# First unit's decays in two loads and two scans, unit 7's decays loaded once, other order numbers

## The chip, the cores and the metric

The kernel runs on one core of one Trainium2 chip. The core has five engines that run at the same time and wait for each other through semaphores: TensorE (PE in the profile), VectorE (DVE), ScalarE (ACT), GpSimd (POOL) and SyncE (SP, which here only issues DMAs). The metric is the device time of one execution in microseconds, as the median of the runs. Lower is better.

## The reference

A linear attention with a decaying state, and behind it a two-layer MLP with an ELU.

```
B, H, S, D = 4, 8, 768, 48
for t in range(S):
    cur = einsum('bhd,bhe->bhde', u[None] * kt, vt)
    y[:, :, t] = einsum('bhd,bhde->bhe', rt, state + cur)
    state = wt[:, :, :, None] * state + einsum('bhd,bhe->bhde', kt, vt)
x = y.transpose(0, 2, 1, 3).reshape(B * S, H * D)      # 3072 x 384
h = x @ w_in                                           # 384 x 2048
g = where(h > 0, h, exp(min(h, 0)) - 1)
out = g @ w_out                                        # 2048 x 384
```

The decays w lie between 0.8 and 0.95.

## The kernel before

**Units and chunks.** The 768 steps are cut into six chunks of 128 steps, each chunk into four units (24 units in all). A unit of the first chunk is one batch row with 128 steps and no state ahead of it ("whole"); a later one is two batch rows with 64 steps each. All eight heads of a unit lie in one tile: 112 partitions, four pairs of heads along the free side.

**What a unit does.** The names are those of the planner's tasks, in brackets the engine.

- `ld_w`, `ld_k`, `ld_v`, `ld_rk` (SP): the loads. w has 521 columns, k and r together 1024.
- `es` (DVE, L442): the running product of the decays from the end of each span of steps to its start, as one scan over reversed columns. The tile `reset` holds a 1 between the spans, so that each starts anew. `gs` (DVE, L451 and L452): the scan in the other direction, which starts from the reciprocals of what `es` ended with.
- `rkc` (DVE, L476): r times k, and `pd` (PE, L481): its product with u, the diagonal. `md` and `sp` (ACT) bring the diagonal into the tile `am`.
- `rh` (DVE, L457): "hats", k and r times the products of the decays, in place.
- `s` (PE, L522, L534, later L509): transposes and scores; `mk` (DVE, L546): the scores above the diagonal into `am`; `kt` (ACT).
- `v` (PE, L509, L574): outputs and the new state. Then `xf`, `xh` (ACT) and `xl` (DVE) make x for the MLP, split into two parts of fewer bits.
- `fl` (ACT, L461): checks each decay against 1, in place, and sums the result; a later branch uses it. For the units below `LATE` = 8, w is loaded once more for this (`ld_wx`) near the middle of the program, into a tile of its own; for the others `fl` runs on w itself, after `gs`, and w's buffer (of two) is held until then.

**The MLP.** Per chunk 16 steps of 128 hidden rows. A step is `g1` (PE, L262 or L266), `r1` and `r2` (ACT: relu and exp), the ELU's last operation (DVE, L276), `gh` (ACT) and `gl` (DVE, L284), and `g2` (PE, L294 or L297). The weights come as 64-bit numbers (`raw`, 768 KB for each of 16 loads) and are converted on chip: two ACT and two DVE operations (L632, L636), then a split into high and low part. The first six are used in the first chunk as they are (`w_f`), with fp32 matmuls of two passes each.

**What sets the order.** The program is put into tasks, and `Plan.order` walks through modelled time: on each engine it takes, of the tasks that are ready and whose buffers are free, the one with the earliest due time plus a number from the table `NUDGE`. The order in which tasks are taken is the order in which the instructions are issued; each engine keeps to it. `FILL` puts a number of products of a tile of ones (L416, into a PSUM bank that nothing reads) ahead of some PE tasks; they are no tasks and need no data.

SP issues each DMA on one of eight semaphores in turn; a ninth load waits until the first has landed.

```
LATE = 8
FILL = {("pd", 0): 15, ("s", 0): 6, ("pd", 1): 8, ("s", 1): 5, ("v", 1): 5, ("pd", 2): 1, ("g1", 2): 5}
```

Of the kernel before, what the change touches and what calls it, by code (L numbers as in the profile page):

```python
# [15 lines left out]
ALU = mybir.AluOpType  # L16
# [16 lines left out]
W1, K1, R1 = CWS + 1, NP * C, NP * C  # L33
WKR = dict(w=(0, W1), k=(W1, W1 + K1 + R1))
# [8 lines left out]
LOW = ['ACT']*16  # L43
RAWS = ["raw0", "raw1", "x1a", "x1b"] * 2 + ["raw0", "raw1"] * 4
DUE = {0: 9.0}
FILL = {("pd", 0): 15, ("s", 0): 6, ("pd", 1): 8, ("s", 1): 5, ("v", 1): 5, ("pd", 2): 1, ("g1", 2): 5}


def _pieces():
    res = []  # L50
    for h in range(H):
        s, e = h * D, (h + 1) * D
        while s < e:
# [16 lines left out]
DMA_FIRST, DMA_ISSUE, DMA_LAT, DMA_RATE = 1.8, 0.47, 1.0, 286.0  # L70
# [17 lines left out]
NUDGE = dict(a={1: -20.75, 2: -37.25},
             cc={1: -10, 2: -20.25, 6: 56.75, 8: -22, 11: 6, 12: 5.75, 14: -4.75, 15: 1.5},
             es={2: -12.5, 4: 3, 6: 3.5, 7: 13.5, 13: -11.5, 16: -1.75, 20: 3.75},  # L90
             g1={3: -1.25, 4: 21, 5: 16.5, 31: -17.25, 37: 70.75, 46: 48.25, 47: -20.75, 48: -0.5, 58: -15.25, 76: -6.25, 80: -9.25, 84: -11.5, 94: -11.75},
             g2={3: 88.5, 18: 4.25, 19: 14.25, 20: -1.5, 26: -11.5, 33: -5.25, 34: -2.75, 42: 0.25, 43: 6, 48: 24, 54: 7.5, 79: -12.75, 83: -8.5, 84: -17.5, 85: 16.75, 87: -4.25, 94: 6.75, 99: 51.75},
             ld={5: -17.75},
             raw={2: -71.5},
             rh={2: -16, 4: -9.75, 8: -40, 9: -5.5, 17: 42, 19: 17.75},
             s={1: -4.25, 12: 31.25, 17: 10},
             sp={1: 13.25, 6: 3.25, 13: -19.75, 19: -3.25, 23: -6},
             v={8: 24.25, 15: -15.5, 16: -18.25},
             wl={1: -22.25, 8: 15.75, 12: -2.25})
KIND = {n: k for k, v in LEADS.items() for n in v.split()}  # L100


class Plan:
# [5 lines left out]
    def add(self, key, eng, dur, fn, after=(), due=None, start=0.0, lock=False, size=0):  # L109
        self.tasks[key] = dict(key=key, eng=eng, dur=dur, fn=fn, after=list(after), due=due, start=start, lock=lock, size=size,  # L110
                               nudge=NUDGE.get(KIND.get(key[0]), {}).get(key[1] if len(key) > 1 else 0, 0.0))

# [215 lines left out]
def rwkv_elu_kernel(ctx, tc, wkr, rk, vp, u, uz, gkrw, gv, gu, wraw, out):  # L328
    nc = tc.nc
# [88 lines left out]
    def load_u(z):  # L418
        nc.sync.dma_start(ubd if z else ub, uz if z else u)

    def load(u_, n):
        i = u_["i"]
        if n in WKR:
            lo, hi = WKR[n]
            t, src = ld.tile([R2, hi - lo], F32, tag=n, name=n, bufs=SLOTS[n]), wkr[i, :, lo:hi]
        elif n == "wx":
            t, src = ld.tile([R2, W1], F32, tag=n, name=n, bufs=SLOTS[n]), wkr[i, :, 0:W1]
        elif n == "rk":
            t, src = ld.tile([P, 2, DM], F32, tag=n, name=n, bufs=SLOTS[n]), rk[i]
        else:  # L430
            t, src = ld.tile([P, 4 * P], F32, tag=n, name=n, bufs=SLOTS[n]), vp[i]
        nc.sync.dma_start(t, src)
        if n == "k":
            u_["k"], u_["r"] = t.rearrange("d (z p t) -> z d p t", z=2, p=NP)
            u_["kr"] = t.rearrange("d (z n) -> d z n", z=2)
        else:
            u_["w" if n == "wx" else n] = t

    def e_scan(u_):
        u_["eg"] = eg = at.tile([R2, 2, CWS + 1], F32, tag="eg", name="eg", bufs=SLOTS["eg"])  # L440
        n = u_["n"]
        nc.vector.tensor_tensor_scan(out=eg[:, 0, 0:n][:, ::-1], data0=u_["w"][:, 1:n + 1][:, ::-1], data1=reset[:, 0, 0:n][:, ::-1],  # L442
                                     initial=0.0, op0=ALU.mult, op1=ALU.max)

    def decay(u_):
        u_["pc"] = pcs[:, u_["i"], 0:NP * C // u_["L"]].unsqueeze(2)
# [232 lines left out]
    for u_ in units:  # L679
        i, c = u_["i"], u_["c"]  # L680
        early = max(0.0, BEGINS[c] - LEAD) if c > 0 else 0.0
        for n, kb in (("w", 274), ("k", 540), ("rk", 462), ("v", 308)):
            if n == "rk" and DIAG[i] == "PE":
                continue
            add(("ld_" + n, i), "SP", DMA_ISSUE, lambda u_=u_, n=n: load(u_, n), start=early, size=kb)
        again = i > 0 and units[i - 1]["whole"] != u_["whole"]
        if again:
            add(("reset", i), "POOL", 1.2, lambda u_=u_: set_reset(nc.gpsimd, u_), [("gs", i - 1)], lock=True)
        add(("es", i), "DVE", K["es"], lambda u_=u_: e_scan(u_), [("const",), ("ld_w", i)] + [("reset", i)] * again, lock=True)
        add(("gs", i), "DVE", K["gs"], lambda u_=u_: g_scan(u_), [("es", i)], lock=True)  # L690
        add(("rh", i), "DVE", K["hat"], lambda u_=u_: hats(u_), [("gs", i), ("ld_k", i)], lock=True)
        add(("pc", i), "ACT", K["pc"], lambda u_=u_: decay(u_), [("es", i)])
        if i < LATE:
            add(("ld_wx", i), "SP", DMA_ISSUE, lambda u_=u_: load(u_, "wx"), [("gs", i)], start=BEGINS[2] + 20.0, due=BEGINS[-3] + 4.0 * i, size=274)
        add(("fl", i), "ACT", K["fl"], lambda u_=u_: flag(u_), [("ld_wx", i)] if i < LATE else [("gs", i)], due=(BEGINS[-3] + 4.0 * i + 20.0) if i < LATE else None)
        if DIAG[i] == "PE":
            add(("rkc", i), "DVE", K["rh"], lambda u_=u_: r_k_rows(u_), [("ld_k", i)], lock=True)
            plan.tasks[("rh", i)]["after"].append(("rkc", i))
            add(("pd", i), "PE", K["pd"], lambda u_=u_: diag_pe(u_), [("rkc", i), ("ubd",)])
            add(("md", i), "ACT", K["md"], lambda u_=u_: diag_out(u_), [("pd", i)])  # L700
        else:
            e = DIAG[i]
            for n, fn, dep in (("rk", r_k, [("ld_rk", i)]), ("rku", r_k_u, [("rk", i), ("ub",)])):
                add((n, i), e, K[n if e == "DVE" else "p" + n],
                    lambda u_=u_, fn=fn, e=e: fn(u_, nc.vector if e == "DVE" else nc.gpsimd), dep, lock=True)
            add(("md", i), "DVE", K["dg"], lambda u_=u_: diag(u_), [("rku", i)])
        if SPREAD[i] == "ACT":
            add(("sp", i), "ACT", K["spa"], lambda u_=u_: spread_act(u_), [("md", i), ("const",)])
        elif SPREAD[i] == "DVE":
            add(("sp", i), "DVE", K["spd"], lambda u_=u_: spread_dve(u_), [("md", i), ("const",)], lock=True)  # L710
        else:
            add(("sp", i), "POOL", K["sp"], lambda u_=u_: spread(u_), [("md", i)], lock=True)
        before = []
        if not u_["whole"]:
            add(("sc", i), "DVE", K["sc"], lambda u_=u_: scale_state(u_), [("pc", i)] + [("up", x["i"]) for x in units[max(0, i - B):i - 1] if set(range(4)[x["b"]]) & set(range(4)[u_["b"]])], lock=True)
            before.append(("sc", i))
        add(("s", i), "PE", K["s0" if u_["whole"] else "s2" if u_["last"] else "s"], lambda u_=u_: score(u_), [("rh", i), ("const",)] + [("sp", i)] * (i > 1) + before, due=DUE.get(i))
        add(("mk", i), "DVE", K["mk0" if u_["whole"] else "mk"], lambda u_=u_: mask(u_), [("s", i), ("sp", i)])
        if not u_["last"]:
            add(("kt", i), "ACT", K["kt"], lambda u_=u_: trans_out(u_), [("s", i)])  # L720
        after = [("mk", i), ("kt", i), ("ld_v", i)]
        if i % B:
            after.append(("v", i - 1))
        add(("v", i), "PE", K["v0" if u_["whole"] else "v2" if u_["last"] else "v"], lambda u_=u_: value(u_), after,
            due=BEGINS[c] - (B - 1 - i % B) * (STAG if c > 1 else STAG1) - 2.0 if c else None)
        if u_["whole"]:
# [256 lines left out]
```

## Time and profile before

| | us |
|---|---|
| median of 3 runs | 508.84 (507.29 to 508.98) |
| the profiled execution, whole | 507.77 |
| its span, first to last instruction | 506.1 |
| ACT busy | 271.7 |
| POOL busy | 41.1 |

In the profile each row of the order in time gives start and length in us, engine, line, operation, what is written and read, and in brackets how long the engine was idle before it and what ended that. A PE row "x30" is 30 passes, since an fp32 product takes two passes. Landing times of DMAs are from issue to the last byte's signal. L416 to L636 are lines of the kernel before; behind line 421 the changed kernel's are 6 to 16 higher.

### The profile page before, as it was taken

How to read it: one execution, taken by the hardware profiler on the slowest of the kernel's cores; microseconds unless marked ns; L12 is line 12 of the kernel's file. 1: busy time of each engine (PE TensorE's matmuls, PEld its weight loads, DVE VectorE, ACT ScalarE, POOL GpSimd, SP SyncE). 2: the span in 40 equal slices, each digit the busy share in tenths (PEclk: the TensorE clock that was granted, in tenths of full speed). 3: DMA queues.
4: the chain of work that ended last, by engine and by line, in shares of the span. 5: the costliest groups of instructions: out<-in, count | busy, mean ns of one | idle time of the engine just before them, and what ended most of it. 6: DMA issues, size and time to landing. Idle time of an engine off the chain costs nothing.

```text
span 506.1 us, 13786 instructions
## 1 busy us (share of the span) xinstructions
PE 499.9 (99%) x6038; PEld 412.7 (82%) x6038; DVE 338.7 (67%) x509; ACT 271.7 (54%) x526; POOL 41.1 (8%) x54
## 2 busy tenths in 40 slices
PE   9999999999999999999999999999999999999996
PEld 8988888887888788888788888888888887888885
DVE  7999999996998423899432899433799543333332
ACT  4989576647554425656544545344645444445352
POOL 2000000013111100112000031100021100000000
PEclk9999999999999999999999999999999999999999
DMA  8967946104813100844290242320332000100001
GB/s 261 354 203 243 301 116 204 68 5 151 234 50 97 51 3 1 242 128 129 65 264 5 81 132 60 100 69 8 115 99 60 3 0 5 63 3 0 1 0 66
DMA packets 18738, 51.09 MB, mean 101 GB/s; under 512 B 2288, under 2 KB 2416, under 8 KB 18672
## 3 DMA queue, kind: packets, MB, share of 16 engines
q1 hardware_dynamic: 18240, 49.36, 32.6%
q8 instruction: 49, 0.80, 0.7%
q10 hardware_dynamic: 432, 0.79, 0.4%
q14 instruction: 17, 0.14, 0.1%
HBM read 45.42 MB, written 4.72 MB: 99 GB/s over the span
## 4 chain that ended last, share of the span: by engine, by line
PE 89%; DVE 6%; DMA 2%; issue 1%; ACT 1%; POOL 0%; DVEq 0%; ACTq 0%; POOLq 0%
PE acc L297 35%; PE ph L266 34%; PE pa L509 6%; PE acc L416 3%; PE acc L294 3%; PE ph L262 2%; PE pa L534 2%; PE pa L574 2%; DMA wx<-in_wkr_dram 2%; PE pb L522 1%; DVE eg L442 1%; DVE m L276 1%; DVE eg L452 0%; PE pb L481 0%; DVE gl L284 0%
## 5 line engine op out<-in xcount | busy, mean ns | idle before, releaser
L276 DVE SCALAR_TENSOR_TENSOR m<-m,ph 128x512 f32<-128x512 f32 (+2 forms) x104 | 66.3, 639 | 84.2 <-ACT m L273 84.0
L270 ACT ACTIVATE m<-ph 128x512 f32<-128x512 f32 (+2 forms) x104 | 58.5, 563 | 94.7 <-PE ph L266 86.7
L266 PE MATMUL ph<-xh,w_l 128*128 128x512 f32 x270 | 105.3, 390 | 0.0
L297 PE MATMUL acc<-gh,w_l 128*128 128x512 f32 x268 | 104.5, 390 | 0.0
L284 DVE TENSOR_TENSOR gl<-m,gh 128x512 fp32r<-128x512 f32 x90 | 62.4, 694 | 41.6 <-ACT gh L280 41.3
L280 ACT CAST gh<-m 128x512 fp32r<-128x512 f32 x90 | 55.7, 619 | 52.0 <-DVE m L276 29.6
L297 PE MATMUL acc<-gh,w_h 128*128 128x512 f32 x180 | 71.8, 399 | 0.0
L266 PE MATMUL ph<-xh,w_h 128*128 128x512 f32 x180 | 71.3, 396 | 0.0
L297 PE MATMUL acc<-gl,w_h 128*128 128x512 f32 x180 | 70.2, 390 | 0.0
L266 PE MATMUL ph<-xl,w_h 128*128 128x512 f32 x180 | 70.1, 390 | 0.0
L273 ACT ACTIVATE m<-m 128x512 f32<-128x512 f32 (+2 forms) x104 | 62.2, 600 | 2.1
L266 PEld LDWEIGHTS ph<-xh,w_l 128*128 128x128 f32 x270 | 50.7, 188 | 10.7
L297 PEld LDWEIGHTS acc<-gh,w_l 128*128 128x128 f32 x268 | 50.3, 188 | 10.7
L502 POOL TENSOR_SCALAR_AFFINE_SELECT am<-md 64x512 f32<-64x512 f32 x32 | 30.1, 942 | 249.0 <-DVE md L471 202.5
L297 PEld LDWEIGHTS acc<-gh,w_h 128*128 128x128 f32 x180 | 33.8, 188 | 7.9
L266 PEld LDWEIGHTS ph<-xh,w_h 128*128 128x128 f32 x180 | 33.8, 188 | 7.8 <-DVE m L276 0.5
L266 PEld LDWEIGHTS ph<-xl,w_h 128*128 128x128 f32 x180 | 33.8, 188 | 6.6
L297 PEld LDWEIGHTS acc<-gl,w_h 128*128 128x128 f32 x180 | 33.8, 188 | 6.5
L266 PE MATMUL ph<-xh,w_g 128*128 128x512 f32 x90 | 36.1, 402 | 0.0
L266 PE MATMUL ph<-xl,w_g 128*128 128x512 f32 x90 | 35.1, 390 | 0.0
L297 PE MATMUL acc<-gh,w_g 128*128 128x512 f32 x88 | 35.0, 398 | 0.0
L297 PE MATMUL acc<-gl,w_g 128*128 128x512 f32 x88 | 34.4, 391 | 0.0
(115 smaller groups left out, 693.8 us busy)
## 6 DMA issues: line engine op xcount, KB each, us to landing
wraw<-in_wraw_dram SPq DMA_DIRECT2D x16, 768.0 KB, 6.7
k<-in_wkr_dram SPq DMA_DIRECT2D x24, 448.0 KB, 6.0
rk<-in_rk_dram SPq DMA_DIRECT2D x20, 384.0 KB, 4.1
v<-in_vp_dram SPq DMA_DIRECT2D x24, 256.0 KB, 6.8
w<-in_wkr_dram SPq DMA_DIRECT2D x24, 227.9 KB, 4.4
out_dram<-o SPq DMA_DIRECT2D x15, 256.0 KB, 2.2
wx<-in_wkr_dram SPq DMA_DIRECT2D x8, 227.9 KB, 2.9
out_dram<-o ACTq DMA_DIRECT2D x3, 256.0 KB, 2.8
```

Source lines behind the costliest of these rows:

```text
L262: nc.tensor.matmul(ph, w_f[f][:, 0, k], x_[2][:, k], start=(k == 0), stop=(k == NK - 1))
L266: nc.tensor.matmul(ph, w[f][:, 0, k], y[:, k], start=(k == n == 0), stop=(k == NK - 1 and n == 2))
L270: act(s["m"], s["ph"], AF.Relu, scale=-1.0)
L273: act(s["m"], s["m"], AF.Exp, scale=-1.0)
L276: stt_(s["m"], s["m"], -1.0, s["ph"], ALU.add, ALU.max)
L280: nc.scalar.copy(s["gh"], s["m"])
L284: nc.vector.tensor_tensor(s["gl"], s["m"], s["gh"].bitcast(F32), ALU.subtract)
L294: nc.tensor.matmul(a_, w_f[f][:, 1, m], fold(s, s["m"][:, a:b]), start=first, stop=final)
L297: nc.tensor.matmul(a_, w[f][:, 1, m], fold(s, g[:, a:b]), start=(first and n == 0), stop=(final and n == 2))
L416: nc.tensor.matmul(pw, ones, ones, start=True, stop=True)
L502: nc.gpsimd.affine_select(out=am[rs].rearrange("t q p s -> t (q p) s"), in_=u_["md"][rs].rearrange("t q p -> t (q p)").unsqueeze(2).broadc ...
L509: nc.tensor.matmul(u_["py"][32 * j:32 * j + 32, h, k], l, r, **flags)
```

## The change

1. Unit 0's w (521 columns) is loaded in two DMAs, columns 259 to 520 first, columns 0 to 258 as a task `ld_w2` of its own. Its scan `es` becomes two scans of 258 columns, the first over the columns that came first. In the planner `es` depends on the first load and `gs` on the second; the instruction that reads columns 1 to 258, the second half of `es`, waits for the second load by its semaphore.
2. `LATE` goes from 8 to 7: unit 7's w is not loaded a second time, and its `fl` runs on w after `gs`.
3. `FILL` and `NUDGE` get other numbers.

```diff
-FILL = {("pd", 0): 15, ("s", 0): 6, ("pd", 1): 8, ("s", 1): 5, ("v", 1): 5, ("pd", 2): 1, ("g1", 2): 5}
+FILL = {("pd", 0): 12, ("s", 0): 5, ("pd", 1): 14, ("s", 1): 4, ("v", 1): 3, ("pd", 2): 1, ("g1", 2): 5}
...
-LATE = 8
+LATE = 7
...
-             es={2: -12.5, 4: 3, 6: 3.5, 7: 13.5, 13: -11.5, 16: -1.75, 20: 3.75},
+             es={2: -38.25, 4: 9.75, 5: -7, 6: -19.75, 7: 22.75, 9: -7.25, 21: -10.75, 22: -12.75},
...
+    def halves(u_):
+        m = u_["n"] // 2 + 1
+        return slice(m, W1), slice(0, m)
+
...
-        nc.sync.dma_start(t, src)
+        cs = halves(u_)[0] if i == 0 and n == "w" else slice(0, hi - lo if n in WKR else None)
+        if n in ("w", "k"):
+            nc.sync.dma_start(t[:, cs], src[:, cs])
+        else:
+            nc.sync.dma_start(t, src)
...
+    def load_rest(u_):
+        cs = halves(u_)[1]
+        nc.sync.dma_start(u_["w"][:, cs], wkr[u_["i"], :, cs])
+
...
-        nc.vector.tensor_tensor_scan(out=eg[:, 0, 0:n][:, ::-1], data0=u_["w"][:, 1:n + 1][:, ::-1], data1=reset[:, 0, 0:n][:, ::-1],
-                                     initial=0.0, op0=ALU.mult, op1=ALU.max)
+        for lo, hi in ((n // 2, n), (0, n // 2)) if u_["i"] == 0 else ((0, n),):
+            nc.vector.tensor_tensor_scan(out=eg[:, 0, lo:hi][:, ::-1], data0=u_["w"][:, lo + 1:hi + 1][:, ::-1], data1=reset[:, 0, lo:hi][:, ::-1],
+                                         initial=0.0, op0=ALU.mult, op1=ALU.max)
...
+        if i == 0:
+            add(("ld_w2", 0), "SP", DMA_ISSUE, lambda u_=u_: load_rest(u_), [("ld_w", 0)], size=137)
+            plan.tasks[("ld_w2", 0)]["after"] = []
...
-        add(("es", i), "DVE", K["es"], lambda u_=u_: e_scan(u_), [("const",), ("ld_w", i)] + [("reset", i)] * again, lock=True)
-        add(("gs", i), "DVE", K["gs"], lambda u_=u_: g_scan(u_), [("es", i)], lock=True)
+        add(("es", i), "DVE", K["es"] + 0.15 * (i == 0), lambda u_=u_: e_scan(u_), [("const",), ("ld_w", i)] + [("reset", i)] * again, lock=True)
+        add(("gs", i), "DVE", K["gs"], lambda u_=u_: g_scan(u_), [("es", i)] + [("ld_w2", 0)] * (i == 0), lock=True)
```

SP's first issues, before (w is loaded for units 0 and 1, then the first raw weights and unit 1's k):

```order
L432 DMA w<-in_wkr_dram 112x521
L432 DMA k<-in_wkr_dram 112x1024
L419 DMA ubd<-in_uz_dram 112x8
L432 DMA w<-in_wkr_dram 112x521
L612 DMA wraw<-in_wraw_dram 128x1536
L432 DMA k<-in_wkr_dram 112x1024
L612 DMA wraw<-in_wraw_dram 128x1536 x2
```

and now:

```order
L438 DMA w<-in_wkr_dram 112x262
L438 DMA k<-in_wkr_dram 112x1024
L449 DMA w<-in_wkr_dram 112x259
L419 DMA ubd<-in_uz_dram 112x8
L625 DMA wraw<-in_wraw_dram 128x1536
L438 DMA w<-in_wkr_dram 112x521
L438 DMA k<-in_wkr_dram 112x1024
L625 DMA wraw<-in_wraw_dram 128x1536 x2
```

The second half of unit 0's w stands third, behind unit 0's k, and unit 1's w (521 columns) has moved behind the first raw weights.

DVE from its first scan on, before. A scan is printed as SCALAR_TENSOR_TENSOR here; eg_155 and k_140 belong to unit 0, eg_168 and k_147 to unit 1:

```order
L442 SCALAR_TENSOR_TENSOR eg_155<-w_138,reset_104 112x516
L451 RECIPROCAL reset_104<-eg_155 112x4
L452 SCALAR_TENSOR_TENSOR eg_155<-w_138,reset_104 112x516
L476 TENSOR_TENSOR rkc_164<-k_140 112x512
L442 SCALAR_TENSOR_TENSOR eg_168<-w_143,reset_104 112x516
L457 TENSOR_TENSOR k_140<-k_140,eg_155 112x1024
L451 RECIPROCAL reset_104<-eg_168 112x4
L452 SCALAR_TENSOR_TENSOR eg_168<-w_143,reset_104 112x516
L476 TENSOR_TENSOR rkc_230<-k_147 112x512
L546 COPY_PREDICATED am_194<-upper_108,pa_218 128x512 x2
L632 SCALAR_TENSOR_TENSOR w_f_98<-w_f_98,wraw_145 128x768
L457 TENSOR_TENSOR k_147<-k_147,eg_168 112x1024
```

and now (eg_152 and k_140 unit 0, eg_220 and k_148 unit 1):

```order
L455 SCALAR_TENSOR_TENSOR eg_152<-w_138,reset_104 112x258 x2
L489 TENSOR_TENSOR rkc_160<-k_140 112x512
L464 RECIPROCAL reset_104<-eg_152 112x4
L465 SCALAR_TENSOR_TENSOR eg_152<-w_138,reset_104 112x516
L470 TENSOR_TENSOR k_140<-k_140,eg_152 112x1024
L455 SCALAR_TENSOR_TENSOR eg_220<-w_146,reset_104 112x516
L464 RECIPROCAL reset_104<-eg_220 112x4
L465 SCALAR_TENSOR_TENSOR eg_220<-w_146,reset_104 112x516
L559 COPY_PREDICATED am_187<-upper_108,pa_209 128x512 x2
L489 TENSOR_TENSOR rkc_233<-k_148 112x512
L645 SCALAR_TENSOR_TENSOR w_f_98<-w_f_98,wraw_144 128x768
L470 TENSOR_TENSOR k_148<-k_148,eg_220 112x1024
```

The r*k product of unit 0 has moved ahead of its second scan, unit 1's first scan behind the hats of unit 0, and the mask of unit 0 ahead of unit 1's r*k product. On PE the sequence of real work is the same up to the middle of the first chunk; of the filling, 12, 5, 14, 4 and 3 products stand where 15, 6, 8, 5 and 5 stood.

ACT in the last third of the first chunk, now (m, ph and gh belong to MLP steps, w_776 is unit 7's w):

```order
L270 ACTIVATE m_1403<-ph_1320 128x512
L273 ACTIVATE m_1403<-m_1403 128x512
L474 ACTIVATE w_776,flags_91<-w_776,lim_105 112x520
L603 CAST xh_1047<-pa_1281 128x2x3x64
L280 CAST gh_1419<-m_1403 128x512
```

Unit 7's `fl` has come in between the exp of one MLP step and its `gh`; its load and `fl` in the middle of the program are gone.

More of the change, by code (lines that the diff above doesn't have):

```diff
@@ L87 @@
              cc="cand cs cb cc cx sg", wl="wh wl wt wl1 wh1", g1="g1 r1 r2 stt", g2="g2 gh gl")
-NUDGE = dict(a={1: -20.75, 2: -37.25},
-             cc={1: -10, 2: -20.25, 6: 56.75, 8: -22, 11: 6, 12: 5.75, 14: -4.75, 15: 1.5},
-             es={2: -12.5, 4: 3, 6: 3.5, 7: 13.5, 13: -11.5, 16: -1.75, 20: 3.75},
[L91 to L99, printed above, removed]
+NUDGE = dict(a={7: 37.25, 12: 6},
+             cc={8: 5.25, 12: 3.5},
+             es={2: -38.25, 4: 9.75, 5: -7, 6: -19.75, 7: 22.75, 9: -7.25, 21: -10.75, 22: -12.75},
+             g1={4: 6.25, 5: 24.5, 6: 23.25, 10: -9.5, 21: -9.5, 32: -15, 36: 57, 45: -32.25, 52: -3.25, 54: 15.5, 57: 7.5, 58: 9.75, 61: -5.75, 64: -10, 71: 23.75, 79: -2.75, 80: -2.75, 81: -6, 84: -2, 86: 23.75, 95: -4, 99: -0.5},
+             g2={3: 105.25, 17: 6, 18: -22, 20: -4.25, 25: 23, 28: 32, 31: 2.5, 33: 20.75, 41: -11.25, 57: 5, 60: 10.25, 70: 20.25, 73: 12.75, 89: 6.25, 90: 36.5},
+             ld={1: -3.5, 20: 14},
+             raw={0: -4.75, 2: -52},
+             rh={2: -15.25, 6: 11.75, 8: -11, 9: -8.25, 14: -7.5, 16: 19, 17: 2.75},
+             s={1: 11.5, 4: -47, 9: 1, 11: 11, 16: -4.25, 22: 5.75},
+             sp={7: 4.25, 10: 22.5, 11: 16.75, 16: 10.5, 18: -7.25, 23: -1},
+             v={8: 6.25},
+             wl={1: -11.75, 15: 8.5})
 KIND = {n: k for k, v in LEADS.items() for n in v.split()}
@@ L684, in rwkv_elu_kernel @@
                 continue
-            add(("ld_" + n, i), "SP", DMA_ISSUE, lambda u_=u_, n=n: load(u_, n), start=early, size=kb)
+            add(("ld_" + n, i), "SP", DMA_ISSUE, lambda u_=u_, n=n: load(u_, n), start=early, size=kb / 2 if i == 0 and n == "w" else kb)
+        if i == 0:
+            add(("ld_w2", 0), "SP", DMA_ISSUE, lambda u_=u_: load_rest(u_), [("ld_w", 0)], size=137)
+            plan.tasks[("ld_w2", 0)]["after"] = []
         again = i > 0 and units[i - 1]["whole"] != u_["whole"]
```

## The prediction

> **What bounds the kernel now.** I read the page first, then the table of waits of PE, then DVE, PE and the DMA issues of the first 50 us in order of time.
>
> ```profile
> PE 499.9 (99%) x6038; PEld 412.7 (82%) x6038; DVE 338.7 (67%) x509; ACT 271.7 (54%) x526; POOL 41.1 (8%) x54
> PE   9999999999999999999999999999999999999996
> DVE  7999999996998423899432899433799543333332
> ```
>
> PE is busy for 499.9 of 506.1 us, in every slice to the last. In the first nine slices (114 us) DVE is nearly full too. PE's waits are few:
>
> ```profile
> PE acc L416 <- POOL ones L383: 1.1, 1, 1.1
> PE ph L262 <- DVE m L276: 0.4, 1, 0.4
> PE pa L509 <- DVE am L548: 0.3, 1, 0.3
> ```
>
> Nothing but 1.8 us of waiting can be won or lost by moving work once PE multiplies without a break. But PE's busy time in the start is partly filling: the 128x128 products of ones (L416), which stand where PE would wait. There PE's real work is paced by DVE, and a gain or loss shows only if DVE's chain moves:
>
> ```profile
> 3.97 1.23 DVE L442 TENSOR_TENSOR_SCAN eg<-w,reset 112x516 f32<-112x516 f32 x1 [1.51 <-DMA w<-in_wkr_dram]
> 5.23 0.18 DVE L451 RECIPROCAL reset<-eg 112x4 f32<-112x4 f32 x1
> 5.45 1.23 DVE L452 TENSOR_TENSOR_SCAN eg<-w,reset 112x516 f32<-112x516 f32 x1
> 6.60 0.67 DVE L476 TENSOR_TENSOR rkc<-k 112x512 f32<-112x512 f32 x1
> 7.18 1.23 DVE L442 TENSOR_TENSOR_SCAN eg<-w,reset 112x516 f32<-112x516 f32 x1
> 8.32 1.20 DVE L457 TENSOR_TENSOR k<-k,eg 112x1024 f32<-112x1024 f32 x1
> 9.44 0.17 DVE L451 RECIPROCAL reset<-eg 112x4 f32<-112x4 f32 x1
> ...
> 11.56 0.69 DVE L476 TENSOR_TENSOR rkc<-k 112x512 f32<-112x512 f32 x1 [0.68 <-DMA k<-in_wkr_dram]
> 12.17 1.34 DVE L546 COPY_PREDICATED am<-upper,pa 128x512 f32<-128x512 uint32 x2
> 13.41 0.94 DVE L632 SCALAR_TENSOR_TENSOR w_f<-w_f,wraw 128x768 uint32<-128x768 uint32 x1
> 14.27 1.21 DVE L457 TENSOR_TENSOR k<-k,eg 112x1024 f32<-112x1024 f32 x1
> ...
> 27.59 0.29 DVE L276 SCALAR_TENSOR_TENSOR m<-m,ph 128x128 f32<-128x128 f32 x1 [0.30 <-ACT m L273]
> ...
> 40.78 0.75 DVE L276 SCALAR_TENSOR_TENSOR m<-m,ph 128x256 f32<-128x256 f32 x2
> ```
>
> From 11.56 us on DVE rests once, 0.30 us before 27.59. PE hangs on it to the end of this stretch, as the chain that ended last shows (start, length, what):
>
> ```profile
> 40.87 0.34 DVE m L276
> 41.21 0.04 issue
> 41.25 1.56 PE ph L262 x6
> ```
>
> Behind 41.25 PE runs on almost without a wait. So the question is how late or early DVE reaches that ELU operation (L276) near 40.8 us.
>
> **The change, part by part.** Starts of operations are read as distances, since DVE starts one before the former's end: scan to reciprocal 1.26 us (3.97 to 5.23), reciprocal to scan 0.22, second scan to the next 1.15 (5.45 to 6.60), r*k product 0.6, hats 1.12 (8.32 to 9.44), mask pair 1.24, one conversion 0.86.
>
> *The two halves.* The rows of the loads, with the time from issue to landing at the end of the lower ones:
>
> ```profile
> 1.28 0.42 SPq L432 DMA_DIRECT2D k<-in_wkr_dram  x1
> 1.74 0.42 SPq L419 DMA_DIRECT2D ubd<-in_uz_dram  x1
> 2.21 0.43 SPq L432 DMA_DIRECT2D w<-in_wkr_dram  x1
> 2.68 0.43 SPq L612 DMA_DIRECT2D wraw<-in_wraw_dram  x1
> 3.15 0.43 SPq L432 DMA_DIRECT2D k<-in_wkr_dram  x1
> ...
> wraw<-in_wraw_dram SPq DMA_DIRECT2D x1, 768.0 KB, 7.1
> ...
> k<-in_wkr_dram SPq DMA_DIRECT2D x1, 448.0 KB, 4.2
> ubd<-in_uz_dram SPq DMA_DIRECT2D x1, 3.5 KB, 4.0
> ...
> w<-in_wkr_dram SPq DMA_DIRECT2D x1, 227.9 KB, 4.6
> ...
> k<-in_wkr_dram SPq DMA_DIRECT2D x1, 448.0 KB, 8.4
> ```
>
> They land in the order of issue: unit 0's k at 5.48 (1.28+4.2), ubd at 5.74, unit 1's w at 6.81, the first raw weights at 9.78, unit 1's k at 11.55. In the changed kernel the second half of unit 0's w is issued third, behind k, and the second half-scan, next on DVE, waits for it. However early the first half lands, that gains nothing: all of DVE is queued behind the second. No row shows this load. It has k's 448 KB ahead of it, so not before 5.5; not later than the next full w, 6.8. I take 5.7, that of ubd, which stands in this third place now. A half-scan costs between 0.62 (half of 1.23) and 0.70 (0.17, what the reciprocal takes on 4 columns, and half of the rest); both give 0.6 to the next start. So: second half-scan 5.7, r*k product 6.3, reciprocal 6.9, second scan 7.1, hats behind it at 8.4, free at 9.5. The diagonal's matmul, now at 7.32, starts at 7.0, and unit 0's scores at 9.7 instead of 9.78. That is the whole gain, and the filling between takes it up.
>
> *What was moved behind it.* Before, unit 1's first scan stood at 7.18, ahead of the hats; now it stands behind them. And its w is issued behind the 768 KB of raw weights. The bytes up to its end are those that had gone by when the raw weights landed, so I take their 9.78 and start the scan at 9.9. Bounds: 9.5, when DVE is free, if w lands as now; 11.6 if it lands as late as k of unit 1. From 9.9: reciprocal 11.16, second scan 11.38, then mask of unit 0 at 12.53, r*k product 13.77, conversion 14.38, hats of unit 1 at **15.24, against 14.27: 0.97 us later**. The 0.68 us that DVE waited for k are gone; what is late next is DVE's own 2.6 us of scans for unit 1, which had lain inside that wait and ahead of it. (By the bounds: 0.6 to 2.7 later.)
>
> *On PE.*
>
> ```profile
> 1.07 6.38 PE L416 MATMUL acc<-ones 128*128 128x128 f32 x30 [1.07 <-POOL ones L383]
> 7.32 1.05 PE L481 MATMUL pb<-ubd,rkc 112*128 112x2 f32 x8
> 8.23 1.58 PE L416 MATMUL acc<-ones 128*128 128x128 f32 x12
> 15.58 0.57 PE L522 MATMUL pb<-ident,k 112*128 112x112 f32 x4
> 17.18 1.08 PE L509 MATMUL pa<-am,v 128*32 128x128 f32 x32
> 18.79 1.38 PE L416 MATMUL acc<-ones 128*128 128x128 f32 x10
> 20.10 1.08 PE L509 MATMUL acc<-am,v 128*32 128x128 f32 x32
> 21.70 1.60 PE L262 MATMUL ph<-xf,w_f 128*128 128x128 f32 x12
> ```
>
> Unit 1's scores follow its hats (15.24+1.21+0.1 = 16.55, now 15.58); scores take 1.6 (15.58 to 17.18), unit 0's values 1.61, three products of filling 0.85 (six passes at 0.13): unit 1's values start at 20.55 and the first layer at 22.15, each 0.45 later. The filling sums to 44 products against 45; the changed counts lie inside these waits, and behind 21.7 they are as before. DVE's order from there to L276 at 27.59 holds the same operations, so DVE is 0.97 late there, less the 0.30 it rested: 0.67, more than PE's own 0.45, hence it decides. To 40.78 the order is the same but for one swap of mask and ELU. **PE is 0.65 late at 41.25** and has no idle time later in which to catch up. (By the bounds: 0.3 to 2.4.)
>
> *Unit 7 and the rest.* The load gone (228 KB near 210 to 250 us) is off PE's path except in the one wait of 0.3 above, at 248.9 us, where ACT had just come from flags that waited for such loads. It gives back 0 to 0.3; I take 0.15. Unit 7's flag moves up, into ACT's work of the first chunk, where PE never waits. Other orders change in nearly every place; with 0.7 us of PE waits left behind 1.1 us, they can gain at most that, and lose what a new wait costs. I take nothing.
>
> Sum: 507.77 (the profiled execution: 506.1 span and 1.7 around it) + 0.65 - 0.15 = 508.3. The median shown is 508.84, 1.07 above that execution; the same step, +0.5, on the median gives **509.3 us**.
>
> **The rivals.**
>
> *It pays.* The second half lands by 5.1 and unit 1's w does not stay behind the raw weights. Then the hats of unit 0 start at 7.8, the scan at 8.9, and unit 1's hats at 14.25: DVE is even with before, and if the 0.3 and 0.4 us waits go as well, 0.5 less: 508.3. For it: the first load did land before the others. Against it: the other landings follow the order of issue, and k's bytes stand ahead.
>
> *Not what it says.* The early part is so buffered that the shift vanishes before 41 us: 508.84. Against it: DVE rests only 0.30 us in 29.
>
> *Slower: PE's slow phase lasts longer.* The first 30 passes take 0.21 us each, the 12 at 8.23 only 0.13: PE starts slow. Now 24 passes end at 1.07+24x0.21 = 6.2, and PE idles until 7.0, where it had no idle. If this keeps it slow through the diagonal and the next filling, these 18 passes cost 0.08 each, 1.4 us; scores of unit 0 move to 11.1, the 28 passes of filling behind them end at 15.9 instead of 14.5, and unit 1's scores and all of PE are 1.2 later than above: +1.7 to the median, 510.5. It decides as soon as the idle time lets the slow phase go on past 9.7. [...]
>
> *Slower: a new wait in the body.* Unit 7's flag is one full-width ACT operation, and the new order sets other masks and ELU operations against PE. Two waits of the size that ACT's flags set now (0.3), or one of 0.9: 510.2.
>
> **How the numbers follow.** Forecast 0.47 (508.6 to 510.0 with the runs' spread), it pays 0.2, not what it says 0.1, slow phase 0.13, new wait 0.1. The runs shown spread from 507.29 to 508.98. The range reaches from the first rival on a low run, 507.4, to the slow phase on a high one, 511.0. What a measurement of this kernel can tell from no change is about 0.5%, 2.5 us: faster than 506.3 needs more than all of PE's waits, 0.02; slower than 511.4 needs the slow phase and a new wait, or w of unit 1 as late as k, 0.06.
>
> **What would show it.** In the changed profile: the second half-scan waits for a DMA until 5.5 to 6; unit 1's first scan starts at 9.8 to 10, after a wait for w; unit 1's hats at 15.2; the first layer at 22.1; PE behind the ELU operation near 41.9. The passes behind the first diagonal at 0.13 us refute the slow phase, at 0.21 they show it. A first layer before 21.7, or a PE wait over 0.5 us behind 50 us, would prove the sum wrong.

## The result and the profile after

| | before | after |
|---|---|---|
| median, 19 runs each | 508.21 us | 511.21 us |
| lowest to highest | 506.82 to 510.71 | 508.00 to 513.54 |
| ratio, 95% interval | | 1.0054 (1.0038 to 1.0071) |
| the profiled execution, whole | 507.77 | 513.44 |
| its span | 506.1 | 511.6 |

The changed kernel is 0.5% slower, and the median lies 0.2 us above the upper end of the predicted range. The 19 executions fall into groups. Seven have a mean granted clock of 0.998 or more and take 508.0 to 508.7 us, but for one of 509.8. Twelve have 0.988 to 0.996 and take 510.8 to 513.5. Two things ask for an explanation: why even the lowest group is above the kernel before, and what the other group is.

The page after, from its busy times and its slices:

```profile
PE 501.0 (98%) x6036; PEld 413.5 (81%) x6036; DVE 339.1 (66%) x510; ACT 272.7 (53%) x526; POOL 45.4 (9%) x54
PE   8799999999999999999999999999999999999996
PEclk9989999999999999999999999999999999999999
```

PE is busy for 1.1 us more, over two passes fewer, and the missing tenths stand in the first two slices. In the third slice the granted clock dips to eight tenths. All of the difference lies in the start: PE's operation behind the ELU near 41 us (41.25 before) comes at 46.79:

```profile
46.79 1.56 PE L262 MATMUL ph<-xf,w_f 128*128 128x256 f32 x6 [0.47 <-DVE m L276]
```

From there to the end of the span it takes 464.8 us, as before (506.1-41.25 and 511.6-46.79).

DVE up to there, in order of time (start, length, operation, idle time before it):

```profile
5.35 0.69 DVE L455 TENSOR_TENSOR_SCAN eg<-w,reset 112x258 f32<-112x258 f32 x1 [1.61 <-DMA w<-in_wkr_dram]
5.96 0.67 DVE L489 TENSOR_TENSOR rkc<-k 112x512 f32<-112x512 f32 x1
...
8.02 1.23 DVE L470 TENSOR_TENSOR k<-k,eg 112x1024 f32<-112x1024 f32 x1
10.84 1.23 DVE L455 TENSOR_TENSOR_SCAN eg<-w,reset 112x516 f32<-112x516 f32 x1 [1.59 <-DMA w<-in_wkr_dram]
...
16.14 1.22 DVE L470 TENSOR_TENSOR k<-k,eg 112x1024 f32<-112x1024 f32 x1
```

The two new waits are where the prediction put them: the second half-scan for its half, unit 1's first scan for its decays. Unit 1's hats are 1.87 us later than before (14.27).

PE over the same time:

```profile
6.68 1.05 PE L494 MATMUL pb<-ubd,rkc 112*128 112x2 f32 x8 [0.69 <-DVE rkc L489]
7.59 1.36 PE L416 MATMUL acc<-ones 128*128 128x128 f32 x10
9.50 0.57 PE L535 MATMUL pb<-ident,k 112*128 112x112 f32 x4 [0.55 <-ACT am L504]
...
15.49 1.03 PE L494 MATMUL pb<-ubd,rkc 112*128 112x2 f32 x8 [1.00 <-DVE rkc L489]
...
22.53 0.43 PE L587 MATMUL acc<-v,kt 128*64 128x48 f32 x8
25.28 0.39 PE L587 MATMUL acc<-v,kt 128*64 128x48 f32 x8 [2.31 <-issue]
25.59 2.83 PE L262 MATMUL ph<-xf,w_f 128*128 128x128 f32 x12
```

Three idle times of 0.5 to 1.0 us are new. Then, in the middle of sixteen like passes (L587), PE stands still for 2.31 us and waits for no semaphore ("issue"). Behind that the first layer's 12 passes take 2.83 us, where before they took 1.60: here PE runs at half rate, a granted clock of 0.50. By stretches of time, each with its length, PE's busy time (instructions), the granted clock, DMA's share and GB/s:

```profile
20.00:25.00 5.00, 2.96 (x70) 1.00 1.05 277
25.00:27.00 2.00, 1.72 (x15) 0.68 1.01 390
27.00:29.00 2.00, 2.00 (x12) 0.50 1.03 235
```

And PE's table of waits, three of its rows:

```profile
PE acc L587 <- issue: 2.3, 1, 2.3
PE pb L494 <- DVE rkc L489: 1.7, 2, 1.0
PE pa L522 <- DVE am L561: 0.5, 1, 0.5
```

The last of them is new: it ends at 111.75 us, and is for a mask. The one of 0.3 us at 248.9 us is gone.

No row says what PE waited for in those 2.31 us. My reading is that it waited for its own instructions, since the DMA page has a queue that is neither a load nor a store:

```profile
q8 instruction: 49, 0.80, 0.6%
```

49 transfers of 16 KB. By the trace's records of single transfers the first of them starts at 22.76 us and takes 1.20 us, and PE goes on at 25.28; in the profile before the first starts at 16.22.

### The profile page after: what moved, and what is told of

It reads as the page before. It is cut to its first block, busy times and chain, and to the rows that moved or that the text cites. A ratio compares the mean times of both kernels' runs of the same rounds, so it can differ in the third digit from the quotient of the medians.

```text
span 511.6 us, 13781 instructions
## 1 busy us (share of the span) xinstructions
PE 501.0 (98%) x6036; PEld 413.5 (81%) x6036; DVE 339.1 (66%) x510; ACT 272.7 (53%) x526; POOL 45.4 (9%) x54
## 4 chain that ended last, share of the span: by engine, by line
PE 83%; DVE 10%; DMA 3%; issue 2%; ACT 1%; SPq 0%; DVEq 0%; ACTq 0%
PE acc L297 34%; PE ph L266 33%; PE pa L522 6%; PE pa L587 2%; PE pa L547 2%; PE ph L262 2%; DMA w<-in_wkr_dram 1%; PE pb L535 1%; PE acc L294 1%; DVE m L276 1%; DMA wraw<-in_wraw_dram 1%; DVE wg L649 1%; DVE eg L455 1%; DVE wg L645 1%; DVE gl L284 1%
## 5 line engine op out<-in xcount | busy, mean ns | idle before, releaser
L515 POOL TENSOR_SCALAR_AFFINE_SELECT am<-md 64x512 f32<-64x512 f32 x32 | 34.1, 1065 | 242.6 <-DVE md L484 218.3
```

The lines of the kernel that those rows point to most:

```text
L515: nc.gpsimd.affine_select(out=am[rs].rearrange("t q p s -> t (q p) s"), in_=u_["md"][rs].rearrange("t q p -> t (q p)").unsqueeze(2).broadc ...
```

## The experiments

Three theories. **Chain:** unit 1's decays behind the raw weights make DVE, and PE behind it, late in every execution. **Clock:** PE's idle times in the start bring it back to half rate in many executions. **Instructions:** PE runs out of instructions since the next block comes late. Each run was timed beside the kernel before on its chip, and left the trace of one execution. The ratios in the tables are the recorded ones and need not be the quotients of the medians beside them.

### Filling up, loads, filling alone, split alone

Run 1, the changed kernel with PE's idle times filled:

```diff
-FILL = {("pd", 0): 12, ("s", 0): 5, ("pd", 1): 14, ("s", 1): 4, ("v", 1): 3, ("pd", 2): 1, ("g1", 2): 5}
+FILL = {("pd", 0): 15, ("s", 0): 7, ("pd", 1): 18, ("s", 1): 4, ("v", 1): 3, ("pd", 2): 1, ("g1", 2): 5}
```

> The changed kernel with more filling at three places: 15, 7 and 18 products instead of 12, 5 and 14, so that PE has none of the idle times of 0.69 us (before unit 0's diagonal), 0.55 us (before its scores) and 1.00 us (before unit 1's diagonal). Theory 'chain' (unit 1's decays, behind the raw weights, make DVE late in every execution): no change, or up to 0.3 us more; lowest executions 508.0 to 508.5. Theory 'clock' (idle time in the start keeps PE at its half rate for longer, in many executions): executions above 509.5 us all but vanish, granted clock 0.998 to 1.0 throughout, median near 508.6. Theory 'instructions' (PE runs dry because its first instruction fetch comes late, at 22.76 us in the profiled execution): the added products are 18 passes more ahead of that point, so PE runs dry no later; executions above 509.5 us stay at least as frequent as 15 in 19, median 511 to 512, and the trace shows an idle time of PE with no semaphore between 20 and 25 us when its fetch starts later than 20 us.

Run 2, the changed kernel with unit 1's decays issued ahead of the first raw weights:

```diff
-        for t in plan.order():
+        order = plan.order()
+        keys = [t["key"] for t in order]
+        order.insert([k[0] for k in keys].index("raw"), order.pop(keys.index(("ld_w", 1))))
+        for t in order:
```

> The changed kernel with one DMA moved: unit 1's decays are issued ahead of the first raw weights again, and land near 6.3 us instead of 10.81. 'Chain': unit 1's first scan starts at 9.2 to 9.3 instead of 10.84, its hats at 14.6 to 15.3 instead of 16.14; the lowest executions fall from 508.0 to 506.8 to 507.3, and the median falls by about 1. 'Instructions': if the late fetch is due to what stands in the DMA queues and not to this load, the executions that are 2.5 to 5 us longer stay, with the same share. 'Clock': the idle time before unit 1's diagonal shrinks or goes, the other two stay: long executions stay, fewer.

Run 3, the kernel before with the changed kernel's `FILL` line:

> The kernel before with the changed kernel's filling and nothing else: 12, 5, 14, 4 and 3 products where 15, 6, 8, 5 and 5 stood. PE then idles about 1.2 us before unit 0's diagonal. 'Clock': executions of 510 to 513 us with a granted clock of 0.988 to 0.996 turn up as in the changed kernel, median 510 or more. 'Chain': as before, 508.2, within 0.4. 'Instructions': as before, since loads and the number of PE's instructions up to 22 us are the same; a fetch at 16 to 17 us and no idle time without a semaphore.

Run 4, the kernel before with the split alone (e_scan as in the change):

```diff
-        nc.sync.dma_start(t, src)
+        if i == 0 and n == "w":
+            t_, src_ = t[:, 259:W1], src[:, 259:W1]
+            u_["w"] = t
+            nc.sync.dma_start(t_, src_)
+        else:
+            nc.sync.dma_start(t, src)
...
             t["fn"]()
+            if t["key"] == ("ld_k", 0):
+                nc.sync.dma_start(units[0]["w"][:, 0:259], wkr[0, :, 0:259])
```

> The kernel before with the split alone: unit 0's decays in two loads, the second behind unit 0's k, scanned in two operations; order, filling and LATE of before, unit 1's decays ahead of the raw weights. 'Chain': the second half-scan waits until 5.3, the first scan's result comes 0.8 us later than in the kernel before, which the 0.68 us that DVE waited for unit 1's k take up but for 0.1 to 0.5; median 508.2 to 508.8. 'Clock': no idle time of PE of more than 0.5 us ahead of 16 us, so no more long executions than the 4 in 19 of the kernel before. 'Instructions': as before as well, fetch at 16 to 17 us.

| run | median (lowest to highest), runs | clock under 0.997 | median before | ratio, 95% interval |
|---|---|---|---|---|
| 1, idle times filled | 509.49 (508.82 to 510.18), 5 | 0 | 507.80 | 1.0038 (1.0025 to 1.0051) |
| 2, w of unit 1 first | 509.61 (507.67 to 514.70), 12 | 5 | 507.80 | 1.0040 (1.0015 to 1.0066) |
| 3, before, new filling | 509.51 (507.66 to 513.19), 9 | 4 | 507.80 | 1.0039 (1.0016 to 1.0062) |
| 4, before, split alone | 510.12 (508.90 to 513.84), 11 | 6 | 507.80 | 1.0058 (1.0032 to 1.0083) |

*Clock* is right about the low clocks. They vanish in run 1 and turn up in runs 3 and 4, where the filling alone, or the split alone, leaves PE idle (for run 4 I had expected no idle time of that size; run 3's median is 0.5 lower than expected). The profile of run 2 shows how, by stretches of time as above:

```profile
6.50:9.00 2.50, 1.99 (x18) 1.00 1.05 330
9.00:10.00 1.00, 0.45 (x4) 0.88 1.05 254
10.00:12.00 2.00, 2.00 (x15) 0.50 0.97 323
12.00:14.00 2.00, 2.00 (x13) 0.50 0.99 397
14.00:17.00 3.00, 3.00 (x17) 0.57 1.04 410
17.00:20.00 3.00, 3.00 (x29) 1.00 1.07 237
```

and PE there:

```profile
9.86 0.98 PE L535 MATMUL pb<-ident,k 112*128 112x112 f32 x4 [0.55 <-ACT am L504]
10.77 2.08 PE L547 MATMUL pa<-k 48*128 48x128 f32 x16
12.78 5.19 PE L416 MATMUL acc<-ones 128*128 128x128 f32 x28
```

PE had already left its slow phase (the filling at 7.95 ran at 0.13 us a pass) and goes back to half the clock near 9.8, until about 16.6: 16 passes take 2.08 us instead of 1.16, and 28 take 5.19 instead of 3.39 (the changed kernel's profile has the shorter times). The clock of 0.88, with half rate at 0.50, puts the start 0.24 us ahead of 10.0, and that of 0.57 the end at 16.6: 6.8 us. In run 4 the half rate starts behind an idle time of 1.31 us:

```profile
8.18 1.05 PE L487 MATMUL pb<-ubd,rkc 112*128 112x2 f32 x8 [1.31 <-DVE rkc L482]
9.09 2.91 PE L416 MATMUL acc<-ones 128*128 128x128 f32 x12
```

and lasts to about 12.5. So it lasts for 3.4 us in run 4 (and in the changed kernel's own profile, from 25.7 to 29.1), and for 6.8 us in run 2 and run 7 (9.65 to 16.5). Ahead of it, from 6.5 to 9.0, PE was busy for 1.99 of 2.5 us in run 2, for 1.95 in run 7 and for 1.19 in run 4, by the profile's modelled ends.

In the same 2.5 us PE was busy for 2.27 in the changed kernel's profile, 2.32 in run 12 and 2.38 in run 9, and the granted clock stayed at 1.00 to 20 us in all three. But the changed kernel's profile has PE busy for only 2.00 of the 3.00 us from 14 to 17, and the clock was 1.00 there and in the 3 us behind. So the busy share of such a stretch does not tell when the clock falls back, and what decides it in one execution and not in the next (5 of run 2's 12 are under 0.997) is not shown. And the changed kernel's own profile has its half rate behind the wait of 2.31 us without a semaphore, not behind the idle times at the start: its low clock has two possible causes. That the idle times at the start do it is shown by run 7, which is the changed kernel up to 11 us and falls to half rate at 9.65 (a clock of 0.82 from 9 to 10 us, of 0.50 from 10 to 14).

*Chain* is not shown by run 2's times. Its five lowest are 507.67 to 508.29, the changed kernel's six lowest 508.00 to 508.73, where I had expected 506.8 to 507.3; and the kernel before was 0.4 lower beside run 2, too (507.80 instead of 508.21). In its trace unit 1's first scan starts at 9.51 instead of 10.84, without a wait, but the mask behind it then waits 0.77 us while PE is at half rate, and the hats come at 15.69. Runs 10 and 11 below bear on *chain* better.

*Instructions* was wrong on run 1 as I put it: its fetch came at 14.73, not late, and PE did not stand still at 22 us. (Its expectation counts 15 executions in 19 of the changed kernel above 509.5 us; there are 13.) But run 1 has no low clock and is still 1.7 us above the kernel before, with two of five above 509.5, where *clock* had expected a median near 508.6. Its trace has a new wait at another place:

```profile
258.15 0.29 PE L587 MATMUL pa<-v,kt 64*64 64x48 f32 x5 [0.60 <-issue]
```

### Both repairs, one idle time at a time

Run 5 is run 2 with run 1's filling; runs 6 and 7 are the changed kernel with more filling at one place (`("pd", 0): 15`, and `("pd", 1): 18`); run 8 is run 5 with `ld_w2` issued ahead of `ld_k` of unit 0.

> The changed kernel with both repairs: unit 1's decays ahead of the first raw weights, and filling of 15, 7 and 18 products in place of 12, 5 and 14. 'Chain' and 'clock' together: unit 1's hats at 14.4 to 14.9, no execution with a granted clock under 0.997, lowest near 507.5, median 507.8 to 508.5, so within 0.3 us of the kernel before or up to 0.7 above it. If 'chain' is wrong the lowest stays at 508.0 to 508.8 and the median at 509.5 as with the filling alone; if 'clock' is wrong, executions of 511 and more stay, about 4 in 10.

> The changed kernel with more filling at one place alone: 15 products instead of 12 before unit 0's diagonal, which closes the idle time of 0.69 us at 6 us; those of 0.55 at 9 us and 1.00 at 14.5 us stay. 'Clock', set off by idle time between 6 and 9.5 us (in two traces the half rate sets in at 9.09 and 9.86): the share of executions above 509.5 us falls from 13 of 19 to under a third. If the wait of 1.00 us before unit 1's diagonal sets it off, the share stays. 'Chain': lowest 508.0 to 508.7 as in the changed kernel.

> The changed kernel with more filling at the other place alone: 18 products instead of 14 before unit 1's diagonal, which closes the idle time of 1.00 us at 14.5 us; those of 0.69 at 6 us and 0.55 at 9 us stay. 'Clock', set off by the idle time between 6 and 9.5 us: the share of executions above 509.5 us stays at half or more, median 510 to 511.5, clocks of 0.988 to 0.996 in about half. If the later idle time sets it off: all but none, median near 508.7.

> As the run with both repairs, and the second half of unit 0's decays issued right behind the first, ahead of unit 0's k. Then the halves land near 2.9 and 3.9 us, the second half-scan ends by 4.6, and the r*k product waits for k (5.5 to 5.6) instead of the second half: 0.3 to 0.5 us earlier on DVE up to unit 1's first scan, and from there the loads of unit 1 decide. 'Chain': 0.2 to 0.4 us under the run with both repairs, 507.5 to 508.1, the same as the kernel before. 'Clock': no clock under 0.997, since PE's filling covers the earlier times too.

| run | median (lowest to highest), runs | clock under 0.997 | median before | ratio, 95% interval |
|---|---|---|---|---|
| 5, both | 510.07 (508.34 to 512.58), 12 | 1 | 507.84 | 1.0042 (1.0025 to 1.0059) |
| 6, idle at 6 us filled | 509.13 (507.75 to 513.85), 12 | 3 | 507.84 | 1.0038 (1.0014 to 1.0062) |
| 7, idle at 14.5 us filled | 509.34 (508.28 to 512.76), 13 | 5 | 507.84 | 1.0014 (0.9994 to 1.0033) |
| 8, halves side by side | 511.68 (510.13 to 513.12), 6 | 1 | 507.84 | 1.0069 (1.0044 to 1.0095) |

Run 5 missed, for two reasons that its trace shows. Unit 1's hats are at 14.62, as expected, but 18 products of filling now hold PE until 15.37, and the first layer starts at 22.80: the filling took the place of the wait. And PE stands still at the same place as in run 1; run 8 too:

```profile
258.57 0.29 PE L587 MATMUL pa<-v,kt 64*64 64x48 f32 x5 [0.83 <-issue]
```

```profile
259.18 0.29 PE L587 MATMUL pa<-v,kt 64*64 64x48 f32 x5 [1.14 <-issue]
```

In all three PE stops behind its pass 3404, and these three have the same number of filling passes. Run 8's halves landed at 2.83 and 3.42, but its r*k product then waited for k to 5.94, and its expectation missed: loading them side by side gains nothing. Its median is 511.68, where 507.5 to 508.1 was expected; the trace's wait of 1.14 us without a semaphore is part of that, and the rest is open. Runs 6 and 7 expected a third or less, and half or more, above 509.5 us; 5 of 12 and 4 of 13 are. The low clocks were 3 of 12 and 5 of 13, too few to tell the idle times apart. Run 7's were 0.995 in four of five, the changed kernel's 0.988 to 0.992 in eight of twelve: shorter, not rarer.

### The number of instructions

Whenever PE stood still without a semaphore in these traces, an instruction transfer had just begun:

| trace | transfer starts | PE goes on | between |
|---|---|---|---|
| after | 22.76 | 25.28 | 2.52 |
| run 1 | 255.76 | 258.15 | 2.39 |
| run 5 | 256.01 | 258.57 | 2.56 |
| run 8 | 256.71 | 259.18 | 2.47 |
| run 3 | 258.95 | 261.58 | 2.63 |

So PE went on 2.39 to 2.63 us after a transfer had begun; that it waits for what the transfer brings, no row says. Where the number of passes ahead is the same, it stops at the same pass (runs 1, 5 and 8); so my reading is that more filling moves the pass at which the next block is needed. Run 9 has run 1's filling time in the changed kernel's number of products:

```diff
+WIDE = {("pd", 0): 160, ("s", 0): 180, ("pd", 1): 164}
...
-    def warm(n):
-        pw = spare()[2][:, 0:P]
+    def warm(n, w=P):
+        pw = spare()[2][:, 0:w]
+        y = ones if w == P else ones[:, 0:w // 2].unsqueeze(1).broadcast_to([P, 2, w // 2])
         for _ in range(n):
-            nc.tensor.matmul(pw, ones, ones, start=True, stop=True)
+            nc.tensor.matmul(pw, ones, y, start=True, stop=True)
...
-            warm(FILL.get(t["key"], 0))
+            warm(FILL.get(t["key"], 0), WIDE.get(t["key"], P))
```

> The changed kernel with as much filling time as the run that had 15, 7 and 18 products, but the changed kernel's own number of products, 12, 5 and 14, made wider (160, 180 and 164 columns in place of 128). So PE has no idle time in the first 15 us, and the number of its instructions is the changed kernel's. In the three traces with 15, 7 and 18 products PE stands still once for 0.8 to 1.35 us without a semaphore, each time at its pass 3404 (near 257 us) and 2.4 to 2.6 us after the start of an instruction fetch. Theory 'clock' alone: median 509.5 as with the 18 passes more. Theory 'instructions' (the wait at pass 3404 comes from where the 16 KB blocks of instructions begin, which 18 more passes move): no wait at pass 3404, nor another without a semaphore, median 508.2 to 508.7, no clock under 0.997 but for one execution in ten or so.

Run 10 is the same on run 2, with 104 columns at the third place:

> As the run with wider filling, with unit 1's decays ahead of the first raw weights too, and products of 104 columns instead of 164 before unit 1's diagonal, since DVE comes 1 us earlier there (with 18 products of 128 the filling itself held PE until 15.4 us). 'Chain', 'clock' and 'instructions' together: the first layer at 21.8 to 22.1, no wait without a semaphore, median 507.6 to 508.1, no different from the kernel before. If unit 1's decays are not what makes DVE late, the median is that of the run with wider filling.

Run 11 is run 10 with 30 passes less:

```diff
-FILL = {("pd", 0): 12, ("s", 0): 5, ("pd", 1): 14, ("s", 1): 4, ("v", 1): 3, ("pd", 2): 1, ("g1", 2): 5}
-WIDE = {("pd", 0): 160, ("s", 0): 180, ("pd", 1): 104}
+FILL = {("pd", 0): 8, ("s", 0): 4, ("pd", 1): 7, ("s", 1): 2, ("v", 1): 2, ("pd", 2): 1, ("g1", 2): 5}
+WIDE = {("pd", 0): 240, ("s", 0): 224, ("pd", 1): 208, ("s", 1): 256, ("v", 1): 192}
```

> As the run before it, with the same filling time in fewer and wider products: 8 of 240 columns, 4 of 224, 7 of 208, 2 of 256 and 2 of 192, which is 30 passes less. 'Instructions': the first fetch starts at a later point of PE's work, still 104 to 108 passes in; whether a wait without a semaphore comes up depends on where the blocks fall now, and if one does, it ends 2.4 to 2.6 us after a fetch has started and costs 0.4 to 1.4 us. 'Clock' and 'chain': the same as the run before it, 507.6 to 508.1, without such a wait.

Run 12, last, is run 9 with one edit:

```diff
-FILL = {("pd", 0): 12, ("s", 0): 5,
-WIDE = {("pd", 0): 160, ("s", 0): 180, ("pd", 1): 164}
+FILL = {("pd", 0): 15, ("s", 0): 5,
+WIDE = {("s", 0): 180, ("pd", 1): 164}
```

> The run with wider filling with one edit: before unit 0's diagonal 15 products of 128 columns instead of 12 of 160, the same time in 6 passes more. In the trace with wider filling PE ran dry at its pass 220 for 1.6 us, its first fetch having started at 22.17; the last pass of filling before unit 1's diagonal is there pass 90, in the run with 15 products at the first place alone pass 96 (fetch at 14.72), with 15, 7 and 18 products pass 108 (14.73 to 14.97). Theory 'instructions': the first fetch is called for some 90 to 104 passes in, so with pass 96 it falls into the filling instead of behind DVE's wait at 15.7, is served at 14.5 to 16 ahead of the long loads, and PE does not run dry at pass 220; clocks stay at 0.998 or more; median 508.4 to 509.1, 1.5 to 2.2 less than with wider filling. If running dry at pass 220 is a single event of one trace and not what makes that run 510.6, the median stays at 510 to 511.

| run | median (lowest to highest), runs | clock under 0.997 | median before | ratio, 95% interval |
|---|---|---|---|---|
| 9, wider filling | 510.61 (508.41 to 512.80), 12 | 0 | 507.62 | 1.0046 (1.0028 to 1.0064) |
| 10, and w of unit 1 first | 510.82 (507.72 to 513.31), 12 | 5 | 507.62 | 1.0048 (1.0022 to 1.0075) |
| 11, 30 passes less | 509.21 (507.67 to 510.78), 12 | 0 | 507.62 | 1.0024 (1.0008 to 1.0041) |
| 12, run 9, 6 passes more | 508.82 (508.33 to 513.40), 12 | 1 | 507.38 | 1.0030 (1.0010 to 1.0049) |

Run 9 did what was expected at pass 3404, where no wait is left, and with the clock, at 0.998 or more in all 12. Yet its median is 510.61, not 508.2 to 508.7. Its trace shows PE standing still without a semaphore where it did in the changed kernel's profile. PE in run 9 (its lines are one or two higher):

```profile
22.77 0.43 PE L589 MATMUL acc<-v,kt 128*64 128x48 f32 x8
24.80 0.38 PE L589 MATMUL acc<-v,kt 128*64 128x48 f32 x8 [1.60 <-issue]
25.12 1.60 PE L263 MATMUL ph<-xf,w_f 128*128 128x128 f32 x12
```

It stops behind pass 220 in both traces: 24+8+10+20+28+8+8+20+32+16+6+32 passes ahead of these eight. The transfer started at 22.17, 2.63 us before PE went on. In the other twelve traces the first transfer starts at 14.7 to 20.6, and none has this wait. Run 12 tests whether that is what makes run 9 slow. My estimate is that the block is called for some 90 to 104 passes in: in run 9 PE had 90 behind it when it came to the wait ahead of 15.73, and no transfer had started; in run 1 the first started at 14.73, some 104 passes in. If so, 6 passes more at the start, in the same time, put that point into the filling, ahead of DVE's wait at 15 us instead of behind it. The transfer starts at 14.81, and PE runs through:

```profile
22.24 0.67 PE L589 MATMUL acc<-v,kt 128*64 128x48 f32 x16
22.83 1.60 PE L263 MATMUL ph<-xf,w_f 128*128 128x128 f32 x12
```

Its median is 508.82, inside the expected 508.4 to 509.1, and ten of twelve lie between 508.33 and 509.32, where nine of run 9's twelve were above 509.9. (The intervals of the two ratios overlap, and the runs were on different chips, whose kernels before differ by 0.24; so this rests on the counts, two against nine above 509.9, and on one trace each.) In run 10 PE still had an idle time of 0.65 us before unit 0's diagonal, and the low clocks stayed; that expectation missed, and five of its executions at full clock lie at 509.5 to 511.0. The trace is that of the lowest of these (0.96 us late at 41 us, and 0.53 for a mask near 107 us); the others stay open. Run 11 has next to none, and no low clock; its first layer is at 21.59 (before: 21.70), but its median is still 1.0024 of the kernel before, and its expectation (507.6 to 508.1) missed too. Its trace is 0.7 us longer than that of the kernel before, by a wait of 0.71 for a mask near 106 us. No version tried beats the kernel before; only run 7's interval includes 1.

## Why the prediction was right or wrong

**Right: what bounds the kernel, and where the cost arises.** From 46.79 us on the sum is the same (464.8 us on both sides), though a wait of 0.5 has come and one of 0.3 has gone. The second half-scan gains nothing, and the hats of unit 0 come 0.3 us earlier (8.02, before 8.32). Unit 1's decays, moved behind 768 KB, make DVE late. No wait of PE is put down to unit 7's flag, and the wait of 0.3 near 248.9 is gone. That the change is slower was forecast too, but most of the 3.0 us came in ways that the sum did not have.

**The term "scan of unit 1 at 9.9" was too small in the profile.** The second half landed at 5.32, ahead of my lower bound of 5.5 (right behind k, at 5.07), but unit 1's decays at 10.81 instead of 9.78. I took the landing of the raw weights for theirs, since the bytes were the same. In fact the raw weights landed at 9.70 with fewer bytes ahead, and the decays came 1.1 us behind them. Over the six traces with this order of loads they land between 8.81 and 11.04, so the term could have come out right in another execution. The hats followed, at 16.14 for 15.24, by the working as given. Two small slips are in that working: 24 passes of 0.21 from 1.07 end at 6.11, not 6.2 (5.99 in the profile), and 20.55 takes six passes of filling for 0.79, where 0.85 stands beside it (0.86 in the profile); with 0.85 the first layer is at 22.21.

Where there is neither half rate nor a wait without a semaphore up to there (the traces of runs 1, 6 and 12), the first layer starts at 22.61 to 22.83, not 22.15, and PE's operation behind the ELU at 42.17 to 42.39, 0.9 to 1.1 us later than before; the prediction said 0.65. In run 6 PE waits for DVE (0.59 before unit 1's diagonal); in run 12 filling and DVE end together, and in run 1, with unit 1's hats at 14.75, the filling holds PE. With unit 1's decays first and no filling in the way (runs 10 and 11) the first layer is at 21.95 and 21.59, and the hats are at 14.50 and 14.62. In run 11 PE's operation behind the ELU is at 41.20, as before; in run 10 it is at 42.21, since DVE rests three times between 16 and 23 us, for 0.97 in all. So that the late decays make PE late in this stretch is shown by run 11's trace, one execution, and no more than likely for the others.

**"I take nothing" for the new order of the rest** missed one wait, of 0.5 in the profile and 0.7 in run 12's, for a mask near 107 to 112 us. It is in seven of the eleven traces with this order (0.29 to 0.74 us), and not in those of runs 1, 5, 7 and 8. I had named a PE wait over 0.5 us behind 50 us as what would prove the sum wrong; it came. For the size of these two terms together there are two readings. Run 12's median, 508.82, is 1.4 above the kernel before on its chip. The seven executions of the changed kernel at full clock have a median of 508.58, 0.4 above the kernel before beside them (508.21). The prediction had 0.5.

**The step that failed was the choice among the rivals: "PE's slow phase lasts longer" at 0.13.** I tied it to idle time that keeps a slow phase going, to be read from the passes behind the first diagonal. These ran at 0.13 us in the profile, which would have refuted it. What happens is another form: PE has left the slow phase and falls back, 0.9 us behind an idle time (run 4) or within the second of two (run 2), for 3.4 or 6.8 us. Over all runs, clocks under 0.997 occur in 40 of the 88 executions of the kernels whose traces have PE idle for 0.8 us or more in all between 2 and 15 us (the changed one and runs 2, 3, 4, 6, 7, 10), in 3 of the 59 of those with 0.7 or less (1, 5, 8, 9, 11, 12; the limit was set after the runs), and in 4 of the 100 executions of the kernel before beside runs 1 to 12. "The filling sums to 44 products against 45; the changed counts lie inside these waits" was the sentence that hid it: the sum was the same, but 0.7, 0.55 and 1.0 us of PE's time were left uncovered in the profile.

**What no rival had:** PE stands still without a semaphore just when an instruction transfer has begun, for 2.31 us in the profile; that it runs out of instructions is my reading. Of the 3.0 us between the medians, 0.4 to 1.4 are the chain and the mask. How the rest divides between clock and instructions can't be said: run 9 took the low clocks away and kept the 3.0 (510.61 against 507.62), and only run 12, whose trace has no wait without a semaphore either, lost half of it. The two seem to stand in for each other. The traces of runs 7 and 9 suggest how: at half rate PE comes to pass 220 at 25.31, at least 4.7 us after the first transfer has started (20.6 at the latest), and at full rate, in run 9, at 22.98, 0.8 us after (22.17). That this is so in the executions without a trace is inferred from their clocks and times.

**Left open:** why the first transfer of instructions starts 14.7 us into one execution and 22.8 into another. The traces show when it starts, not when it was called for. The loads of that time are in flight in all of them.

## What to carry to other kernels

Filling that stands for waiting had three measures here, not one: its time had to cover the waits (the clock was under 0.997 in 40 of 88 executions of the kernels whose traces have PE idle for 0.8 us or more, in 3 of 59 of those with 0.7 or less); it must not outlast them, or it takes their place (run 5: PE held until 15.37 us); and with its number of instructions went the pass behind which PE stood still without a semaphore (220 in two traces, 3404 in three), by my reading for the next of its instructions. In this kernel an edit that shifted starts by a microsecond would have needed all three set anew. And where one execution's profile is read, the granted clocks and times of all executions say first whether it stands for them.

## What was not expected of the hardware

- PE's clock fell back to half after it had once come up, although PE had been busy for 1.99 of 2.5 us ahead of it, and stayed there for 6.8 us (run 2, 9.8 to 16.6 us; from 9.86 on PE was never idle).
- The changed kernel's trace has 49 instruction transfers of 16 KB (0.80 MB), and in six traces PE stood still without a semaphore until 2.39 to 2.63 us after the start of one. With six short passes more at the start of the program a median was 508.82 us instead of 510.61 (0.24 of this lies between the kernels before on the two chips).
- The same loads in the same order land up to 2.2 us apart from one execution to the next (unit 1's decays, 8.81 to 11.04).
